# A Strassen second product in a pooled-attention and GELU-MLP kernel on one core

## The chip, the core and the metric

The kernel runs on one core of a Trainium2 chip. TensorE (PE) multiplies matrices and writes only to PSUM; VectorE (DVE), ScalarE (ACT) and GpSimd (POOL) do elementwise work, each from its own queue in program order; SyncE's queue (SP) issues nearly all DMAs, also in order. The metric is the device time of the core in microseconds, lower is better.

## The reference

For each of 8 batches with 8 heads, 576 queries of 64 elements attend to keys and values that are averaged over runs of 8 (72 pooled keys per head). The result, 4608 tokens of 512, goes through an MLP with 2048 hidden units and a tanh GELU.

```python
k_p = k.reshape(B, H, Sp, pool, D).mean(axis=3)
v_p = v.reshape(B, H, Sp, pool, D).mean(axis=3)
scores = scale * np.matmul(q, k_p.transpose(0, 1, 3, 2))
attn = softmax(scores)                       # over the 72 pooled keys
x = np.matmul(attn, v_p)                     # then (B*S, H*D)
h = x @ w_in                                 # 512 -> 2048
g = 0.5 * h * (1.0 + np.tanh(c * (h + 0.044715 * h * h * h)))
out = g @ w_out                              # 2048 -> 512
```

## The kernel before

**Tiling.** The tokens go in nine groups of 512. Groups 0 to 7 are the first 512 tokens of a batch each; the ninth, R, gathers the last 64 tokens of all eight batches. The order is `seq = [0, 1, ..., 6, R, 7]`; below, "group n" counts places in this order, 0 to 8. Weights stay in SBUF as bf16 (`w_in_b`, `w_out_b`), and so does the hidden activation of the current group, `gT` (128 partitions x 16 chunks x 512 tokens). Everything of the reference is computed with bf16 matmuls into float32 PSUM.

**A group's MLP**, `mlp` (line 368). First product: for each of 16 chunks `fo` of the hidden units, `hidden` (340) issues 4 matmuls of 512 columns into one PSUM bank, and ACT writes the GELU into `gT` (346). Second product: for each of 4 quarters of the tokens, 16 matmuls of 512 columns (`output`, 360) with `gT` as the stationary operand, then a VectorE copy out of PSUM (`finish`, 363) and a store. Group 0 has its own order (`mlp_first`), which works in token halves of 256 columns (`hidden_half`, 348) in its first product. The last group cuts its last quarter into column pieces (line 388).

**Work of the next group in between.** `mlp` calls `hook(s)` ahead of matmul number s of the group (its *slot*: 0 to 63 in the first product, 64 to 127 in the second), and what is registered there is emitted at this place in the program order of all engines. The schedule is written by hand (`manual_schedule`), so that a slot fixes the order in each engine's queue, and semaphores do the rest. The attention of group n+1 is registered in group n as follows:

- slot 12 (26 in group 1): `pool(b, 0, 5)`, three float32 additions on VectorE (132 to 134) of k and the first part of v over the 8 elements of a run, `dup_k`, and the transpose of the pooled keys by DMA from SP (184);
- slot 32: `pool(b, 5, 9)`, and at 33 `spread_v` on GpSimd (154), which lays the pooled v out block-diagonally in `vbd`;
- slot 56: `k_spread`, two VectorE copies into `kbd`; slot 57: the load of q for group n+2;
- slots 67, 69, 78, 82: four `scores` (214, 4 matmuls each) and `exps` on ACT (229); the PSUM tag `sc` has two tiles;
- slots 79, 82, 86, 90: four `norm` (sum 236, reciprocal 245, multiply 248; the second one's multiply on GpSimd), each followed by a DMA transpose of the result from SP (278);
- slot 91: `cast_q` of group n+2 on GpSimd, its DMA transpose (205), and `load_kv` of group n+2, the load of k and v (99, 94, 92); slot 92: a part of R's q (115);
- slot 121: `values` (298), 16 matmuls of 512 columns (310; for R 64 of 64 columns, 319), and two ACT copies into `xT`, the moving operand of the next group's first product.

Each pooling uses the kv tile that was loaded in the group before. Groups 1 to 5 load such a tile; group 7 needs no pooling, since the batch of the last group was pooled for R. The PSUM tag `mm` has four banks, which hidden chunks and output quarters take in turn.

**Staging.** `w_in` and `w_out` arrive as float32 in tiles of the tag `kv` (three buffers, shared with the k and v loads) and are cast to bf16 during group 0.

Of the kernel before, what the change touches and what calls it, by code (L numbers as in the profile page):

```python
# [19 lines left out]
def kernel(  # L20
# [36 lines left out]
    kvp = ctx.enter_context(tc.tile_pool(name="kvp", bufs=3))  # L57
# [168 lines left out]
    def exps(g, j):  # L226
        sc = st[g].pop(("sc", j))
        e = work.tile([128, H, Sp], F32, name="e", bufs=4)
        nc.scalar.activation(out=e.rearrange("p (x h) s -> p x (h s)", x=2), in_=sc[:, :, 0:4 * Sp],  # L229
                             func=ACT.Exp, scale=1.0 / 64.0)  # L230
# [49 lines left out]
    def xT_tile(g):  # L280
        st[g]["xT"] = work.tile([128, KO, MAIN], BF16, name="xT")
# [81 lines left out]
    def finish(g, r, o, eng):  # L363
        osb = work.tile([128, DM], F32, name="osb", bufs=4)
        copy(eng, osb, o)
        store(g, r, osb)

    def mlp(g, hooks, last):
# [5 lines left out]
        for r in range(4):  # L374
            if last and r == 3:
                break
            o = psum.tile([128, DM], F32, name="mm", tag="mm", bufs=4)
            for fo in range(FO):
                hook(64 + 16 * r + fo)
                output(g, r, fo, o)  # L380
            finish(g, r, o, nc.vector)
        if last:

            osb = work.tile([128, DM], F32, name="osb", bufs=4)
            for i, (c0, c1) in enumerate([(0, 256), (256, 384), (384, 512)]):
                o = psum.tile([128, DM], F32, name="mm", tag="mm", bufs=4)
                for fo in range(FO):
                    nc.tensor.matmul(out=o[:, 0:c1 - c0], lhsT=gT[:, fo, 384:512], rhs=w_out_b[:, fo, c0:c1],  # L388
                                     start=(fo == 0), stop=(fo == FO - 1))
                copy(nc.vector, osb[:, c0:c1], o[:, 0:c1 - c0])  # L390
                store(g, 3, osb, c0, c1, nc.scalar if i == 1 else nc.sync)
# [211 lines left out]
    for n_, g in enumerate(seq):  # L603
        if n_ == 0:
            continue
        hooks = {}
        if n_ + 1 < len(seq):
# [16 lines left out]
            for j in range(4):  # L624
                sj = ([67, 67, 80, 80] if n == R else [67, 69, 78, 82])[j]
                at(hooks, sj, scores, n, j)
                at(hooks, sj, exps, n, j)
# [4 lines left out]
            tail_of_attention(hooks, n, 121)
        if n_ + 2 < len(seq):
# [4 lines left out]
            at(hooks, 91, cast_q, n2, 0, 4, nc.gpsimd)  # L638
            at(hooks, 91, qT_tile, n2)
            at(hooks, 91, q_transpose_dma, n2)  # L640
            at(hooks, 91, load_kv, n2)
        if n_ == 1:
            at(hooks, 92, q_tile, R)
        if 1 <= n_ <= 4:
            at(hooks, 92, load_q, R, n_ - 1, n_, nc.sync)
        mlp(g, hooks, n_ + 1 == len(seq))
# [30 lines left out]
```

The softmax here doesn't subtract the row's maximum and nothing guards it: scores larger than these inputs give would overflow.

## Time and profile before

| | us |
|---|---|
| median of 3 runs | 294.53 (294.53 to 294.56) |
| span of the profiled execution | 292.6 |
| group 0's start to the first matmul of group 1 | 52.1 |
| first matmul of groups 2, 3, 4, 5, 6 | 82.14, 111.98, 141.83, 171.73, 201.57 |
| first matmul of groups 7 and 8 | 232.05, 261.89 |
| first 128-column piece of the last group to the last matmul's end | in 286.06 to 289.76 |
| granted TensorE clock | 1.000 |
| VectorE busy in group 3, first and second product | 7.13 of 13.82, 8.52 of 16.03 |
| GpSimd busy in group 3, first and second product | 2.51, 3.51 |

The span is the time from the first to the last instruction of one profiled execution; the runs' times include what lies around it. The lines of a timeline below give start, length, engine, kernel line, operation, output and inputs with shapes, and the count of instructions merged; in brackets stands how long the engine sat idle before it, and what ended that. `SPq` is the SP queue's issue of a DMA. `PEld` is a weight load.

### The profile page before, as it was taken

How to read it: one execution, taken by the hardware profiler on the slowest of the kernel's cores; microseconds unless marked ns; L12 is line 12 of the kernel's file. 1: busy time of each engine (PE TensorE's matmuls, PEld its weight loads, DVE VectorE, ACT ScalarE, POOL GpSimd, SP SyncE). 2: the span in 40 equal slices, each digit the busy share in tenths (PEclk: the TensorE clock that was granted, in tenths of full speed). 3: DMA queues.
4: the chain of work that ended last, by engine and by line, in shares of the span. 5: the costliest groups of instructions: out<-in, count | busy, mean ns of one | idle time of the engine just before them, and what ended most of it. 6: DMA issues, size and time to landing. Idle time of an engine off the chain costs nothing.

```text
span 292.6 us, 4562 instructions
## 1 busy us (share of the span) xinstructions
PE 284.2 (97%) x1712; PEld 142.8 (49%) x1739; DVE 141.8 (48%) x236; ACT 156.4 (53%) x233; POOL 64.7 (22%) x86
## 2 busy tenths in 40 slices
PE   8899999999999999999999999999999999999996
PEld 3678753445444544454445444544444544444444
DVE  5892778076517460757065806481639100920012
ACT  1586574777067706671567257724673377436500
POOL 4575443222303040114002400240024000100000
PEclk9999999999999999999999999999999999999999
DMA  7999999996699369945994599148944900451012
GB/s 234 354 386 347 380 381 201 340 257 168 149 298 278 102 134 288 251 142 133 268 283 150 126 250 299 15 113 243 293 146 103 183 23 2 85 112 38 0 72 72
DMA packets 73301, 56.32 MB, mean 192 GB/s; under 512 B 45888, under 2 KB 55488, under 8 KB 73280
## 3 DMA queue, kind: packets, MB, share of 16 engines
q1 hardware_dynamic: 73136, 55.98, 69.6%
q8 instruction: 13, 0.21, 0.3%
q10 hardware_dynamic: 144, 0.07, 0.1%
q14 instruction: 8, 0.07, 0.1%
HBM read 36.70 MB, written 9.44 MB: 158 GB/s over the span
## 4 chain that ended last, share of the span: by engine, by line
PE 81%; DMA 8%; DVE 4%; SPq 3%; ACT 1%; issue 1%; POOL 0%; ACTq 0%
PE mm L360 37%; PE mm L344 36%; DMA w_out_s<-in_moe_w_out_dram 5%; DMA w_in_s<-in_moe_w_in_dram 3%; PE xo L310 3%; PE sc L214 2%; SPq L437 2%; DVE eb L248 1%; ACT gT L346 1%; PE mm L388 1%; DVE den L236 1%; SPq L99 1%; PE xo L319 1%; DVE kv L132 0%; DVE kv L133 0%
## 5 line engine op out<-in xcount | busy, mean ns | idle before, releaser
L360 PE MATMUL mm<-w_out_b,gT 128*128 128x512 bf16 x543 | 125.9, 379 | 1.4 <-issue 0.8
L344 PE MATMUL mm<-xT,w_in_b 128*128 128x512 bf16 x502 | 111.4, 379 | 0.5
L346 ACT ACTIVATE gT<-mm 128x512 bf16<-128x512 f32 x128 | 76.4, 597 | 38.4 <-PE mm L344 38.4
L360 PEld LDWEIGHTS <-gT 128*128 128x128 bf16 x560 | 53.1, 98 | 60.3 <-issue 3.1
L344 PEld LDWEIGHTS <-w_in_b 128*128 128x128 bf16 x512 | 50.1, 98 | 60.5 <-issue 0.3
L81 DVE COPY osb<-mm 128x512 f32<-128x512 f32 (+2 forms) x37 | 24.2, 657 | 58.9 <-PE mm L360 52.8
L79 ACT CAST xT<-xo 128x1024 bf16<-128x1024 f32 (+1 forms) x18 | 16.6, 967 | 56.6 <-PE xo L310 48.2
L154 POOL TENSOR_TENSOR vbd<-kvb,vmask 128x256 bf16<-128x256 bf16 (+2 forms) x40 | 21.5, 561 | 105.1 <-DVE kvb L134 104.9
L236 DVE TENSOR_REDUCE den<-e 128x8 f32<-128x576 f32 x36 | 26.5, 736 | 36.8 <-ACT e L229 36.8
L132 DVE TENSOR_TENSOR kv<-kv 128x1024 f32<-128x1024 f32 (+3 forms) x19 | 21.8, 1149 | 38.4 <-DMA kv<-in_v_dram 32.3
L229 ACT ACTIVATE e<-sc 128x576 f32<-128x576 f32 x36 | 22.4, 650 | 9.6 <-ACT e L229 4.1
L248 DVE TENSOR_TENSOR eb<-e,r 128x576 bf16<-128x576 f32 x24 | 23.3, 972 | 0.8
L81 POOL CAST q_b<-q_sb 128x2048 bf16<-128x2048 f32 (+2 forms) x9 | 17.4, 1937 | 14.5 <-DMA q_sb<-in_q_dram 14.5
L248 POOL TENSOR_TENSOR eb<-e,r 128x576 bf16<-128x576 f32 x6 | 6.9, 1150 | 57.3 <-ACT e L229 30.4
L355 PE MATMUL mm<-xT,w_in_b 128*128 128x256 bf16 x128 | 15.5, 273 | 0.2 <-DVE xT L81 0.2
L214 PE MATMUL sc<-kbd,qT 128*128 128x144 bf16 x128 | 13.3, 226 | 0.4 <-ACT qT L79 0.2
L214 PEld LDWEIGHTS <-qT 128*128 128x128 bf16 x128 | 9.9, 98 | 7.3 <-issue 0.7
L355 PEld LDWEIGHTS <-w_in_b 128*128 128x128 bf16 x128 | 12.1, 98 | 1.8 <-issue 0.3
L133 DVE TENSOR_TENSOR kv<-kv 128x512 f32<-128x512 f32 (+3 forms) x19 | 12.4, 651 | 0.7
L357 ACT ACTIVATE gT<-mm 128x512 bf16<-128x512 f32 x16 | 9.5, 597 | 5.9 <-PE mm L355 5.8
L558 ACT ACT_TABLE_LOAD x8 | 10.3, 1283 | 0.1
L81 POOL CAST w_in_b<-w_in_s 128x512 bf16<-128x512 f32 (+1 forms) x10 | 8.6, 874 | 2.4 <-DMA w_in_s<-in_moe_w_in_dram 2.4
(62 smaller groups left out, 123.5 us busy)
## 6 DMA issues: line engine op xcount, KB each, us to landing
out_dram<-osb SPq DMA_DIRECT2D x31, 256.0 KB, 6.8
kv<-in_k_dram SPq DMA_DIRECT2D x7, 1024.0 KB, 7.6
q_sb<-in_q_dram SPq DMA_DIRECT2D x7, 1024.0 KB, 6.2
kv<-in_v_dram SPq DMA_DIRECT2D x6, 1024.0 KB, 9.2
w_in_s<-in_moe_w_in_dram SPq DMA_DIRECT2D x8, 512.0 KB, 9.8
w_out_s<-in_moe_w_out_dram SPq DMA_DIRECT2D x4, 1024.0 KB, 13.7
kv<-in_v_dram SPq DMA_DIRECT2D x4, 512.0 KB, 10.2
out_dram<-osb SPq DMA_DIRECT2D x9, 128.0 KB, 2.4
```

The costliest lines, as they stand in the source:

```text
L79: eng.copy(out=out, in_=in_)
L81: eng.tensor_copy(out=out, in_=in_)
L132: add(out=t[:, :, 0:4, :], in0=t[:, :, 0:4, :], in1=t[:, :, 4:8, :], op=ALU.add)
L154: eng.tensor_tensor(out=vbd[p0:128, b, n0:n1, :].rearrange("p (c r) (hh d) -> p c (r hh) d", c=max(m, 1), d=D), in0=kvb[p0:128, 4 + c0:4 + ...
L214: nc.tensor.matmul(out=o, lhsT=qT[:, j, pr, :], rhs=kbd[:, g, pr].rearrange("d hh s -> d (hh s)"), start=True, stop=True)
L229: nc.scalar.activation(out=e.rearrange("p (x h) s -> p x (h s)", x=2), in_=sc[:, :, 0:4 * Sp], func=ACT.Exp, scale=1.0 / 64.0)
L236: nc.vector.reduce_sum(out=den, in_=e, axis=AX.X)
L248: eng.tensor_tensor(out=o.rearrange("p (h s) -> p h s", s=Sp), in0=e, in1=r.unsqueeze(2).to_broadcast([128, H, Sp]), op=ALU.mult)
L344: nc.tensor.matmul(out=hp, lhsT=w_in_b[:, ko, fo * 128:(fo + 1) * 128], rhs=st[g]["xT"][:, ko, :], start=(i == 0), stop=(i == KO - 1))
L346: nc.scalar.activation(out=gT[:, fo, :], in_=hp, func=ACT.Gelu_apprx_tanh)
L355: nc.tensor.matmul(out=hp[:, f, :], lhsT=w_in_b[:, ko, (fo + f) * 128:(fo + f + 1) * 128], rhs=st[g]["xT"][:, ko, c0:c0 + 256], start=(ko ...
L360: nc.tensor.matmul(out=o, lhsT=gT[:, fo, r * 128:(r + 1) * 128], rhs=w_out_b[:, fo, :], start=(fo == 0), stop=(fo == FO - 1))
```

## The change

**The second product of groups 1 to 8** is computed by Strassen's scheme in Winograd's form. `gT` is seen as a 2 x 2 matrix of blocks: token halves (256 columns each) by even and odd chunks (a11, a12 for the first half, a21, a22 for the second). `w_out_b` likewise: even and odd chunks by left and right 256 output columns (b11 to b22). Instead of 64 matmuls of 512 columns there are seven products, in the order 1, 2, 6, 5, 7, 3, 4, of 2 x 8 matmuls of 256 columns each, so that the second product has 112 slots (64 to 175).

- `w_sums` builds four sums of w_out's blocks once (`tw`): two on GpSimd at slot 168 of group 0, two on VectorE at slots 2 and 6 of group 1.
- `g_sums` builds, for each group and each pair of chunk pairs, s3 = a11 - a21, s1 = a21 + a22 (in place, over a21), s2 = s1 - a11 and s4 = a12 - s2: four bf16 additions of 2 x 256 elements, at slots 18, 34, 50 (all on VectorE) and 65 (s3 on GpSimd).
- Three PSUM banks accumulate: x takes products 1, 6, 7, 4; y takes 2; z takes 5, 3. Between them VectorE and ACT copy intermediate sums into `keep` or add them into `osb`: x after 1 (VectorE) and after 6 (ACT), z after 5 (ACT). Output goes out in two stores per group, after products 3 and 4.

**The first product of groups 2 to 8** begins with its first four chunks by token halves (`hidden_half`, 32 matmuls of 256 columns), then goes on in 512. **The values** are cut into halves to match (`values_part`): the first half at slot 156 of the group before, the second at slot 4 of the group itself, and each is copied by ACT and VectorE, one half each.

**Slots and buffers.** The attention's slots in the second product are spread over the new count: scores at 68, 71, 92, 100; norms at 81, 97, 104, 114; cast of q, q's transpose and `load_kv` at 116. The tag `kv` has two buffers instead of three, and a constant tile `stage` takes the second half of each weight and later the sums s2 to s4 and `keep`. `kvb` and `xT` have one buffer instead of two, `e` three instead of four.

```diff
-    kvp = ctx.enter_context(tc.tile_pool(name="kvp", bufs=3))
+    kvp = ctx.enter_context(tc.tile_pool(name="kvp", bufs=2))
...
+    NP = FO // 2
+    HN = DM // 2
+    tw = consts.tile([128, 4, NP, HN], BF16, name="tw")
+    stage = consts.tile([128, 4096], F32, name="stage")
+    sums_ = stage[:, 0:3072].bitcast(BF16).rearrange("p (i m t) -> p i m t", i=3, m=NP)
+    keep = stage[:, 3072:4096].rearrange("p (i c) -> p i c", i=2)
+    wq = w_out_b.rearrange("p (m e) c -> p m e c", e=2)
+    gq = gT.rearrange("p (m e) t -> p m e t", e=2)
...
-            st[b]["kvb"] = work.tile([128, NB, 2, D], BF16, name="kvb")
+            st[b]["kvb"] = work.tile([128, NB, 2, D], BF16, name="kvb", bufs=1)
...
-        e = work.tile([128, H, Sp], F32, name="e", bufs=4)
+        e = work.tile([128, H, Sp], F32, name="e", bufs=3)
...
-        st[g]["xT"] = work.tile([128, KO, MAIN], BF16, name="xT")
+        st[g]["xT"] = work.tile([128, KO, MAIN], BF16, name="xT", bufs=1)
...
+    def values_part(g, half, engs):
+
+        xo = psum.tile([128, 2, 2, 256], F32, name="xo", tag="sc", bufs=2)
+        eT = st[g]["eT"]
+        for x in range(2):
+            if g < B:
+                for part, rows_ in ((SMALL, 32), (BIG, 64)):
+                    for pr in (x, x + 2):
+                        for hh in range(2):
+                            r0, c = part[2 * pr + hh]
+                            n = dict(PARTS[pr])[c]
+                            nc.tensor.matmul(out=xo[64 * hh:64 * hh + 64, pr // 2, x, :],
+                                             lhsT=vbd[r0:r0 + rows_, g, n, 64 * hh:64 * hh + 64],
+                                             rhs=eT[r0:r0 + rows_, 2 * half:2 * half + 2, c, :],
+                                             start=(part is SMALL), stop=(part is BIG))
+                continue
+            for pr in (x, x + 2):
+                for b in range(4 * half, 4 * half + 4):
+                    p0 = 64 * (b % 2)
+                    t0 = 64 * (b - 4 * half)
+                    for y, (c, n) in enumerate(PARTS[pr]):
+                        nc.tensor.matmul(out=xo[:, pr // 2, x, t0:t0 + 64], lhsT=vbd[:, b, n, :],
+                                         rhs=eT[:, b // 2, c, p0:p0 + 64], start=(y == 0), stop=(y == 1))
+        for k in range(2):
+            copy(engs[k], st[g]["xT"][:, 2 * k:2 * k + 2, 256 * half:256 * half + 256], xo[:, k])
...
+    def osb_tile():
+        return work.tile([128, 2, DM], F32, name="osb")
...
+    def w_sums(which, m0, m1, eng):
+
+        b11, b12, b21, b22 = [wq[:, m0:m1, i, HN * h:HN * h + HN] for i in range(2) for h in range(2)]
+        t = [tw[:, i, m0:m1] for i in range(4)]
+        in0, in1 = [(b12, b11), (b22, t[0]), (b22, b12), (b21, t[1])][which]
+        eng.tensor_tensor(out=t[which], in0=in0, in1=in1, op=ALU.subtract)
+
+    def g_sums(m0, eng3):
+
+        a11, a12, a21, a22 = [gq[:, m0:m0 + 2, i, 256 * h:256 * h + 256] for h in range(2) for i in range(2)]
+        s2, s3, s4 = [sums_[:, i, m0:m0 + 2] for i in range(3)]
+        eng3.tensor_tensor(out=s3, in0=a11, in1=a21, op=ALU.subtract)
+        nc.vector.tensor_tensor(out=a21, in0=a21, in1=a22, op=ALU.add)
+        nc.vector.tensor_tensor(out=s2, in0=a21, in1=a11, op=ALU.subtract)
+        nc.vector.tensor_tensor(out=s4, in0=a12, in1=s2, op=ALU.subtract)
...
+    def mlp(g, hooks, last, split):
         hook = runner(hooks)
-        for fo in range(FO):
+        if split:
+            for half in range(2):
+                for fo in (0, 2):
+                    hidden_half(g, fo, half, lambda s: hook(s // 2) if s % 2 == 0 else None, 16 * half + 4 * fo)
...
+        y, z = bank(), bank()
+        x = psum.tile([128, 2, MAIN], F32, name="x2", tag="sc", bufs=2)[:, :, 0:HN] if last else bank()
+        osb = [osb_tile(), osb_tile()]
+        add = nc.vector.tensor_tensor
+        lhs = {1: (gq, 0, 0), 2: (gq, 1, 0), 4: (gq, 1, 256), 5: (gq, 0, 256)}
+        for n, (prod, acc, fresh) in enumerate([(1, x, 1), (2, y, 1), (6, x, 0), (5, z, 1), (7, x, 0), (3, z, 0), (4, x, 0)]):
+            for p in range(2):
+                for m in range(NP):
+                    hook(64 + 16 * n + 8 * p + m)
+                    if prod in lhs:
+                        t, e, c = lhs[prod]
+                        lt = t[:, m, e, c + 128 * p:c + 128 * p + 128]
+                    else:
+                        lt = sums_[:, {6: 0, 7: 1, 3: 2}[prod], m, 128 * p:128 * p + 128]
+                    rt = {1: lambda: wq[:, m, 0, 0:HN], 2: lambda: wq[:, m, 1, 0:HN], 3: lambda: wq[:, m, 1, HN:DM],
+                          4: lambda: tw[:, 3, m], 5: lambda: tw[:, 0, m], 6: lambda: tw[:, 1, m], 7: lambda: tw[:, 2, m]}[prod]()
+                    nc.tensor.matmul(out=acc[:, p, :], lhsT=lt, rhs=rt, start=bool(fresh and m == 0 and (p == 0 or (last and acc is x))),
+                                     stop=(m == NP - 1), skip_group_check=True)
+                if last and prod == 4:
+                    copy(nc.vector, osb[1][:, p, 0:HN], x[:, p])
+                    nc.sync.dma_start(out=out[g * S:g * S + MAIN, :].rearrange("(t j) c -> t j c", j=4)[:, 2 + p, 0:HN],
+                                      in_=osb[1][:, p, 0:HN])
+            left, right = [slice(HN * i, HN * i + HN) for i in range(2)]
+            k0, k1 = [keep[:, i].rearrange("p (r c) -> p r c", r=2) for i in range(2)]
+            if prod == 1:
+                copy(nc.vector, k0, x)
+            elif prod == 2:
+                add(out=osb[0][:, :, left], in0=y, in1=k0, op=ALU.add)
+            elif prod == 6:
+                copy(nc.scalar, k0, x)
+            elif prod == 5:
+                copy(nc.scalar, k1, z)
+            elif prod == 7:
+                add(out=osb[1][:, :, right], in0=x, in1=k1, op=ALU.add)
+                if last:
+                    store_pair(g, 1, osb[1], HN, DM)
+            elif prod == 3:
+                add(out=osb[0][:, :, right], in0=z, in1=k0, op=ALU.add)
+                store_pair(g, 0, osb[0])
+            elif not last:
+                copy(nc.vector, osb[1][:, :, left], x)
+                store_pair(g, 1, osb[1])
...
+    for which in (0, 2):
+        at(hooks, 168, w_sums, which, 0, NP, nc.gpsimd)
...
+        for i in range(4):
+            at(hooks, [18, 34, 50, 65][i], g_sums, 2 * i, nc.gpsimd if i == 3 else nc.vector)
+        if n_ == 1:
+            at(hooks, 2, w_sums, 1, 0, NP, nc.vector)
+            at(hooks, 6, w_sums, 3, 0, NP, nc.vector)
...
-                sj = ([67, 67, 80, 80] if n == R else [67, 69, 78, 82])[j]
+                sj = 64 + ([4, 4, 30, 34] if n == R else [4, 7, 28, 36])[j]
                 at(hooks, sj, scores, n, j)
                 at(hooks, sj, exps, n, j)
                 if j == 0:
-                    at(hooks, 79, eT_tile, n)
-                at(hooks, [79, 82, 86, 90][j], norm, n, j, nc.gpsimd if j == 1 else nc.vector)
-                at(hooks, [79, 82, 86, 90][j], e_transpose_dma, n, j)
-            tail_of_attention(hooks, n, 121)
+                    at(hooks, 64 + 17, eT_tile, n)
+                nj = 64 + [17, 33, 40, 50][j]
+                at(hooks, nj, norm, n, j, nc.gpsimd if j == 1 else nc.vector)
+                at(hooks, nj, e_transpose_dma, n, j)
+            at(hooks, 64 + 66, nc.scalar.preload_act_table_set, GELU_SET)
+            at(hooks, 64 + 92, xT_tile, n)
+            at(hooks, 64 + 92, values_part, n, 0, [nc.scalar, nc.vector])
+        if n_ > 1:
+            at(hooks, 4, values_part, g, 1, [nc.scalar, nc.vector])
...
-            at(hooks, 91, cast_q, n2, 0, 4, nc.gpsimd)
-            at(hooks, 91, qT_tile, n2)
-            at(hooks, 91, q_transpose_dma, n2)
-            at(hooks, 91, load_kv, n2)
+            at(hooks, 64 + 52, cast_q, n2, 0, 4, nc.gpsimd)
+            at(hooks, 64 + 52, qT_tile, n2)
+            at(hooks, 64 + 52, q_transpose_dma, n2)
+            at(hooks, 64 + 52, load_kv, n2)
...
-        mlp(g, hooks, n_ + 1 == len(seq))
+            at(hooks, 64 + 53, load_q, R, n_ - 1, n_, nc.sync)
+        mlp(g, hooks, n_ + 1 == len(seq), n_ > 1)
```

More of the change, by code (lines that the diff above doesn't have):

```diff
@@ L363, in finish, with store_pair @@
     def finish(g, r, o, eng):
[L364 to L368, printed above, removed]
-        hook = runner(hooks)
-        for fo in range(FO):
+        osb = osb_tile()
+        copy(eng, osb[:, 0, :], o)
+        store(g, r, osb[:, 0, :])
+    def osb_tile():
+        return work.tile([128, 2, DM], F32, name="osb")
+    def store_pair(g, half, osb, c0=0, c1=DM, eng=nc.sync):
+        if g < B:
+            dst = out[g * S:g * S + MAIN, :].rearrange("(p j) c -> p j c", j=4)[:, 2 * half:2 * half + 2, c0:c1]
+            eng.dma_start(out=dst, in_=osb[:, :, c0:c1])
+        else:
+            for b in range(4):
+                r0 = (4 * half + b) * S + MAIN
+                p0 = 64 * (b % 2)
+                eng.dma_start(out=out[r0:r0 + 64, :], in_=osb[p0:p0 + 64, b // 2])
+    def w_sums(which, m0, m1, eng):
[11 more added lines that the diff above has]
+    def mlp(g, hooks, last, split):
+        hook = runner(hooks)
+        if split:
+            for half in range(2):
+                for fo in (0, 2):
+                    hidden_half(g, fo, half, lambda s: hook(s // 2) if s % 2 == 0 else None, 16 * half + 4 * fo)
+        for fo in range(4 if split else 0, FO):
             hidden(g, fo, hook, 4 * fo)
@@ L373, in mlp, with bank @@
             nc.scalar.preload_act_table_set(EXP_SET)
[L374 to L391, printed above, removed]
+        def bank():
+            return psum.tile([128, 2, HN], F32, name="mm", tag="mm", bufs=4)
@@ new lines, in mlp @@
+        y, z = bank(), bank()
[10 more added lines that the diff above has]
+                        lt = t[:, m, e, c + 128 * p:c + 128 * p + 128]
+                    else:
+                        lt = sums_[:, {6: 0, 7: 1, 3: 2}[prod], m, 128 * p:128 * p + 128]
[27 more added lines that the diff above has]
+                store_pair(g, 1, osb[1])
@@ L433 @@
         if c % 2 == 0:
-            w_in_s.append(kvp.tile([128, KO, 1024], F32, name="w_in_s", tag="kv"))
+            w_in_s.append(kvp.tile([128, KO, 1024], F32, name="w_in_s", tag="kv") if c == 0 else
+                      stage.rearrange("p (k f) -> p k f", k=KO))
         o = 512 * (c % 2)
@@ L448, in w_out_load @@
         if c % 2 == 0:
-            w_out_s[c // 2] = kvp.tile([128, 8, DM], F32, name="w_out_s", tag="kv")
+            w_out_s[c // 2] = (kvp.tile([128, 8, DM], F32, name="w_out_s", tag="kv") if c == 0 else
+                               stage.rearrange("p (f c) -> p f c", f=8))
         t = w_out_s[c // 2][:, 4 * (c % 2):4 * (c % 2) + 4, :]
@@ L637 @@
                 at(hooks, 57, load_q, n2, 0, 4, nc.sync)
[L638 to L641 removed]
+            at(hooks, 64 + 52, cast_q, n2, 0, 4, nc.gpsimd)
+            at(hooks, 64 + 52, qT_tile, n2)
+            at(hooks, 64 + 52, q_transpose_dma, n2)
+            at(hooks, 64 + 52, load_kv, n2)
         if n_ == 1:
[L643 removed]
+            at(hooks, 64 + 53, q_tile, R)
         if 1 <= n_ <= 4:
[L645 to L646 removed]
+            at(hooks, 64 + 53, load_q, R, n_ - 1, n_, nc.sync)
+        mlp(g, hooks, n_ + 1 == len(seq), n_ > 1)
 _INS = ['q', 'k', 'v', 'moe_w_in', 'moe_w_out']
```

## The prediction

> **What bounds the kernel now.** I read the page's busy shares first, then the timelines of the four engines and of the SP queue over one middle group. The page says:
>
> ```profile
> PE 284.2 (97%) x1712; PEld 142.8 (49%) x1739; DVE 141.8 (48%) x236; ACT 156.4 (53%) x233; POOL 64.7 (22%) x86
> ```
>
> PE is busy nearly all the time, VectorE (DVE) half. TensorE's timeline of group 3, and the one stretch where 256-column matmuls run alone (start, length, engine, line, count):
>
> ```profile
> 23.06 9.01 PE L355 MATMUL mm<-xT,w_in_b 128*128 128x256 bf16 x81
> ...
> 109.35 1.18 PE L310 MATMUL xo<-eT,vbd 32*64 32x512 bf16 x16
> 110.46 1.69 PE L360 MATMUL mm<-w_out_b,gT 128*128 128x512 bf16 x7
> 111.98 13.98 PE L344 MATMUL mm<-xT,w_in_b 128*128 128x512 bf16 x62
> 125.80 0.81 PE L360 MATMUL mm<-w_out_b,gT 128*128 128x512 bf16 x3
> 126.44 0.41 PE L214 MATMUL sc<-kbd,qT 128*128 128x144 bf16 x4
> ```
>
> The first product takes 125.80 - 111.98 = 13.82 us for 64 matmuls, 0.216 each. The group's period is 29.85 (111.98 to 141.83). A 256-column matmul costs (9.01 - 0.27, the last one's length) / 80 = 0.109, with a weight load for each: the load stays hidden. PE has no gap, so PE bounds this kernel. But VectorE and the SP queue run in a loop beside it, and the reader should see how little slack that loop has. First the SP queue (issues), then VectorE:
>
> ```profile
> 107.68 1.33 SPq L205 DMA_TRANSPOSE qT<-q_b  x1
> 109.06 1.30 SPq L99 DMA_DIRECT2D kv<-in_k_dram  x1
> ...
> 133.24 4.18 SPq L278 DMA_TRANSPOSE eT<-eb  x3
> 137.52 1.71 SPq L205 DMA_TRANSPOSE qT<-q_b  x1
> 139.28 1.20 SPq L99 DMA_DIRECT2D kv<-in_k_dram  x1
> ```
>
> ```profile
> 117.71 1.49 DVE L132 TENSOR_TENSOR kv<-kv 128x1280 f32<-128x1280 f32 x1 [4.83 <-DMA kv<-in_v_dram]
> ...
> 120.80 1.42 DVE L132 TENSOR_TENSOR kv<-kv 128x1024 f32<-128x1024 f32 x1
> 122.25 0.69 DVE L133 TENSOR_TENSOR kv<-kv 128x512 f32<-128x512 f32 x1
> ...
> 124.82 0.93 DVE L81 COPY kbd<-kTd 64x288 bf16<-64x288 bf16 x2 [1.42 <-DMA kTd<-kvb]
> 128.65 0.75 DVE L236 TENSOR_REDUCE den<-e 128x8 f32<-128x576 f32 x1 [2.90 <-ACT e L229]
> ...
> 134.83 1.36 DVE L248 TENSOR_TENSOR eb<-e,r 128x576 bf16<-128x576 f32 x1
> ```
>
> The loop: the kv load is issued at 109.06; VectorE waits 4.83 us for it and pools from 117.71; scores, exponentials and four norms follow, the last ending at 134.83 + 1.36 = 136.19; the SP queue, in order, issues the last transpose of e, then that of q (137.52), and only then the next kv load at 139.28. Load to load is 30.2 us, of which only 1.42 + 2.90 = 4.3 are waits that can close up. The bare loop is thus 25.9 us, against a PE period of 29.85.
>
> **What the Trainium skill says.** "VectorE: DVE Perf Modes", section on the perf-mode tier table: an all-bf16 tensor_tensor out of SBUF runs two elements a cycle, 1224 ns for 2048 elements against 2293 ns in float32. The trace has no all-bf16 tensor_tensor on VectorE; its float32 one of 512 elements (0.69 us) and of 1280 (1.49) fit the page's one-a-cycle rate with about 151 cycles fixed. "SBUF — State Buffer", section "Who interferes with whom": a VectorE instruction with two SBUF inputs and a GpSimd instruction that reads SBUF exclude each other. The trace agrees: the norm's multiply takes 0.76 alone and 1.36 beside GpSimd's 2.42 us cast of q. "TensorE: Matmul & The Clock Gate", section "Back-to-back issue gap": 262 cycles for 256 columns, the 0.109 above.
>
> **The change, part by part.**
>
> *TensorE.* 64 matmuls of 0.216 (13.82) become 112 of 0.109 (12.23): -1.59 a group, eight groups, -12.7. The first four chunks of the first product, in halves, are 32 x 0.109 instead of 16 x 0.216: +0.04, seven groups, +0.3. The values: 16 matmuls took 1.11 (109.35 to 110.46); now 32 of half the columns, between 0.56 and 1.11 per 16; I take 0.6, so +0.1 a group, +0.7. Unhindered, a middle group is 29.85 - 1.59 + 0.04 + 0.1 = 28.4 us.
>
> *ACT.* Two PSUM copies more, 0.60 each by the 512-element rows, and half of the xT copy goes to VectorE: it has 1 us or so to spare at each product. Nothing. *PSUM.* Bank x is read out after products 1 and 6 while products 2 and 5 (1.75 us each) run; enough for a 0.69 copy if the copying engine is free.
>
> *VectorE, the part that decides.* g_sums adds 15 additions of 512 bf16 elements (one more on GpSimd, about 1.0 from its 576-element row of 1.15, hidden unless VectorE is early). Bounds: 0.33 if the fixed part is 58 cycles (the same page's errata table), 0.69 if the float32 rate held. I take (256 + 151) / 0.96 = 0.42, and 0.45 start to start, since s1, s2 and s4 depend on each other: 1.8 for four, 1.35 for three. They stand in VectorE's program order behind the pooling from group 2 on: slot 12 pools, slots 18, 34 and 50 are sums, slot 65 the last sums. So they can't fill the wait for kv. They are queued behind it, and behind them stand k_spread, the copy of product 1, the norms, and through SP the next kv load. The kv load still stands behind the norms and q's transpose (slot 116 against 114). The new loop, in order:
> - kv issue to pooling 8.4 (117.71 - 109.06 = 8.65 here; five groups give 7.4 to 9.2)
> - pooling of five chunks 3.1 (117.71 to 120.80), sums 1.8, pooling of four 2.6
> - sums beside spread_v, which holds GpSimd 2.1 us: 1.8 + 0.3 (0 to 1.6); sums 1.8
> - k_spread 0.8; last three sums 1.35
> - copy of product 1: 0.65
> - norms with one PSUM eviction among them 7.5 (128.65 to 136.19)
> - last e transpose 1.3, q transpose 1.8 (136.19 to 139.28 = 3.1)
>
> Sum 33.2. The short way agrees: 25.9 + 6.75 + 0.65 = 33.3. This exceeds the 28.4 that PE needs, so the loop sets the pace. PE will be seen waiting in product 6, which needs s2 and the emptied bank x: they come about 4.5 us late. That wait could lower the granted clock afterwards (the page's clock-gate part names idle windows of some 3.4 us); PE then has slack, so it costs 0 to 1.7 us once, at the end of the loop; I take 0.
>
> *GpSimd and group 1.* w_sums puts two 2048-element additions on GpSimd, about 3.7 us each by the slope between its 256- and 576-element rows, from 49.9 to 57.3; VectorE's two w_sums need their results and end near 58.6, just as the kv data lands (58.58). Then: sums 1.8, pooling 3.1, sums 1.8, pooling 2.6, sums 2.1, k_spread 0.8, sums 1.35, copy 0.65, norms 7.5, SP 3.1: the kv load goes out at 83.4 (before: 79.78). If w_sums are free: 81.6.
>
> *Stores, tile counts.* Fewer, larger stores behind the loads as before; buffers cut from 3 to 2 or 2 to 1 are released a group earlier than needed (kv(n+2) overwrites a tile pooled in the preceding group). Nothing; if that cover were missing, a load would be later still.
>
> *Sum.* Loads go out in groups 1 to 5; the loop repeats four times: 83.4 + 4 x 33.2 = 216.2. The sixth group pools 7.7 later (no part of the remainder's q is loaded with it) and reaches the emptied bank after 3.1 + 1.8 + 2.6 + 2.1 + 1.8 + 0.8 + 1.35 + 0.65 = 14.2, at 238.1; five products of 1.75, scores and the remainder's 32 value matmuls (half of 2.03) are 10.1: 248.2, where before stood 232.05. The seventh (no pooling) runs at PE's pace, 28.9 with its own value matmuls: 277.1. The last is 13.85 + 0.6 + 12.23 = 26.7: 303.8. The tail, before 292.6 - 289.76 = 2.9: span 306.7. The median of the runs is 294.53 - 292.6 = 1.9 above the profiled span: **308.6 us**.
>
> **Rivals.**
> A, faster: the loop hides under PE. Then 294.5 - 12.7 + 0.3 + 0.7 = 282.8. It needs a loop below 28.4, 4.8 us less than my sum. For it: VectorE is only 48% busy, and with 15 x 0.45 more per group some 70%. Against: busy share counts for nothing in a chain that waits 8.4 us for its data. The kernel becomes faster than before where the loop is below about 30.6, since the end moves some 5.5 us per us of loop and mine lies 14.1 above the old time.
> B, the loop binds but barely: additions at 0.33 (-1.8), loads at 7.4 (-1.0), no GpSimd interference (-0.3): 30.1, giving about 291.5; with the middle of these, 31.5, about 299. For it: each end is within its bounds. Against: all at once.
> C, the additions run at the float32 rate, 0.69 + 0.04: +4.2 per loop, 37.4: 308.6 + 5.5 x 4.2 = 332. For it: the pattern is two runs of 256 with a gap, and one is in place. Against: both runs are contiguous 16-bit.
> D: PE's 256-column stream in the second product does not hide its weight loads (98 ns each): against it stands 0.109 over 81 matmuls with the same kind of loads.
>
> **How the numbers follow.** The forecast (loop 32 to 35, 302 to 318) has 0.62; A 0.10; B 0.14, of which 0.03 is faster, 0.02 the same and the rest slower; C 0.12; D 0.02. The range 297 to 325 takes in B's upper half and the interference bound of 1.6 (x 5.5 = 9), and leaves out A and most of C. Within 0.2% (0.6 us) is about what a measurement can't tell from no change. Faster 0.13, same 0.02, slower 0.85.
>
> **What would show it.** In the changed kernel's trace: 256-column matmuls at 0.109 in the second product; a PE gap of 3 to 5 us per group before product 6, released by VectorE; VectorE without idle time from pooling to the last norm; the kv load issued after the group's end instead of 2.9 us ahead of it, and 33 us from the one before; bf16 additions at 0.42. I am wrong if PE runs through (A), if additions are 0.69 (C), or if the kv load goes out before the norms.

## The result, and the profile after

The changed kernel takes 341.07 us (median of four runs, 339.48 to 341.83), the kernel before 294.53 on the same chip: 1.157 times as long, 95% interval 1.153 to 1.160. The forecast said slower, by 14; it is 46.5. The profiled execution spans 340.0 us against 292.6. The page of the changed kernel:

```profile
PE 294.6 (87%) x2289; PEld 200.4 (59%) x2299; DVE 215.6 (63%) x379; ACT 161.0 (47%) x249; POOL 86.0 (25%) x96
...
PE   8889994697999499948999699939998699999995
...
DVE  5875680597738784396739773888449954483532
...
PEclk9999998597999789996999799969999599999999
...
DVE 35%; PE 32%; DMA 20%; SPq 8%; issue 4%; POOL 1%; ACT 1%; DVEq 0%; POOLq 0%
```

The first line is busy time by engine, the next three are the span in 40 slices (tenths busy, and the granted TensorE clock), the last is the chain that ended last, by engine. TensorE (PE) held 81% of that chain before and holds 32% now; VectorE (DVE) and DMA hold 55%. In groups 1 to 6 PE falls to between 3 and 6 tenths, and the clock falls there or in the slice behind. The first such hole, in slices 7 and 8, is the widest.

The windows view, one line for group 1, one for group 2 and one for group 7 (stretch, its length, busy time of PE, PEld, DVE, ACT and GpSimd with counts, granted clock, DMA share, GB/s):

```profile
52.44:95.06 42.62, 32.14 (x209) 19.92 (x208) 26.73 (x43) 17.31 (x27) 15.34 (x11) 0.84 0.52 140
95.06:132.41 37.35, 32.06 (x241) 22.10 (x240) 24.96 (x42) 17.07 (x26) 7.91 (x8) 0.91 0.66 164
278.83:308.35 29.52, 29.16 (x258) 21.07 (x257) 16.89 (x33) 16.96 (x26) 2.30 (x2) 1.00 0.21 59
```

Groups 1 to 8 took 30.04, 29.84, 29.85, 29.90, 29.84, 30.48, 29.84 and 30.71 us before. After, they take 42.62, 37.35, 37.99, 35.07, 37.11, 36.25, 29.52 and 31.65. So group 1 gives +12.6, groups 2 to 6 give +33.9, groups 7 and 8 together +0.6, and the start +0.3: 47.4. Group 7, which pools nothing, is the only one that gained. The loss lies in two places, the loop of groups 2 to 6 and a separate delay in group 1.

**The loop.** SP's issues around the second product of group 2, then VectorE, then PE:

```profile
93.85 1.29 SPq L108 DMA_DIRECT2D kv<-in_k_dram  x1
...
122.10 7.56 SPq L287 DMA_TRANSPOSE eT<-eb  x4
129.77 1.81 SPq L214 DMA_TRANSPOSE qT<-q_b  x1
131.63 1.11 SPq L108 DMA_DIRECT2D kv<-in_k_dram  x1
```

```profile
102.77 1.49 DVE L141 TENSOR_TENSOR kv<-kv 128x1280 f32<-128x1280 f32 x1 [4.38 <-DMA kv<-in_v_dram]
...
106.50 0.42 DVE L429 TENSOR_TENSOR gT<-gT 128x512 bf16<-128x512 bf16 x1
...
113.40 1.19 DVE L429 TENSOR_TENSOR gT<-gT 128x512 bf16<-128x512 bf16 x1
...
115.42 0.46 DVE L90 COPY kbd<-kTd 64x288 bf16<-64x288 bf16 x2
...
119.66 0.69 DVE L90 COPY stage<-mm 128x512 f32<-128x512 f32 x1 [2.40 <-PE mm L463]
```

```profile
110.33 0.60 PE L463 MATMUL mm<-w_out_b,gT 128*128 128x256 bf16 x4
115.94 0.64 PE L223 MATMUL sc<-kbd,qT 128*128 128x144 bf16 x4 [5.01 <-DVE kbd L90]
...
117.49 4.38 PE L463 MATMUL mm<-w_out_b,gT 128*128 128x256 bf16 x21
...
129.28 1.00 PE L345 MATMUL xo<-eT,vbd 32*64 32x256 bf16 x16
130.22 0.61 PE L463 MATMUL mm<-w_out_b,stage 128*128 128x256 bf16 x4
```

The kv load goes out at 131.63, 0.8 us ahead of the group's end at 132.41 (2.9 ahead before), and 37.8 us after the one before it (30.2). VectorE waits for the load, pools, and works without a gap to 117.3. PE issues four matmuls of product 1 and then stops for 5.01 us, ahead of the scores and not ahead of product 6: the scores need `kbd`, and k_spread stands behind two rounds of sums in VectorE's order. Soon after the stop, 21 matmuls of 256 columns take from 117.49 to 121.70, 4.2 us, where 21 x 0.109 is 2.3. VectorE in turn stands idle for 2.40 us until PE has finished product 1. So each of the two waits for the other once per group.

**Group 1.** The waits view of the changed kernel (who waits for whom: us in all, times, the longest), summed over the whole span:

```profile
DVE xT L90 <- ACT xT L88: 25.4, 14, 2.1
...
PE sc L223 <- DVE kbd L90: 23.2, 5, 6.1
...
DVE stage L90 <- PE mm L463: 10.9, 5, 2.4
...
DVE osb L90 <- DMA out_dram<-osb: 11.3, 1, 11.3
...
PE mm L379 <- DVE osb L90: 7.9, 1, 7.9
```

The second and third lines are the loop's pair: five times in five groups. The last two occur once, at 50 to 62 us. Group 0's four output evictions went into four `osb` tiles before; now each takes one of two tiles of twice the size. The third waits 11.3 us for the store of the tile that it takes over, which stands in SP's queue behind the kv load, and PE waits 7.94 us for the PSUM bank that this eviction would empty.

### The profile page after: what moved, and what is told of

The parts are those of the page before. It is cut to its first block, busy times and chain, and to the rows that moved or that the text cites. A ratio compares the mean times of both kernels' runs of the same rounds, so it can differ in the third digit from the quotient of the medians.

```text
span 340.0 us, 5749 instructions
## 1 busy us (share of the span) xinstructions
PE 294.6 (87%) x2289; PEld 200.4 (59%) x2299; DVE 215.6 (63%) x379; ACT 161.0 (47%) x249; POOL 86.0 (25%) x96
## 4 chain that ended last, share of the span: by engine, by line
DVE 35%; PE 32%; DMA 20%; SPq 8%; issue 4%; POOL 1%; ACT 1%; DVEq 0%; POOLq 0%
PE mm L463 16%; DMA kv<-in_v_dram 10%; PE mm L379 7%; DVE kv L141 5%; DMA kv<-in_k_dram 4%; DVE gT L429 4%; DVE den L245 4%; DVE eb L257 3%; DMA out_dram<-osb 3%; DVE kv L142 3%; DVE stage L430 3%; SPq L214 3%; DMA q_sb<-in_q_dram 2%; SPq L108 2%; DVE stage L428 2%
## 5 line engine op out<-in xcount | busy, mean ns | idle before, releaser
L379 PE MATMUL mm<-xT,w_in_b 128*128 128x512 bf16 x392 | 89.5, 385 | 8.5 <-DVE osb L90 7.9
L379 PEld LDWEIGHTS <-w_in_b 128*128 128x128 bf16 x400 | 39.7, 99 | 55.6 <-issue 11.4
L390 PE MATMUL mm<-xT,w_in_b 128*128 128x256 bf16 x352 | 43.4, 273 | 1.8 <-DVE xT L90 1.8
L463 PEld LDWEIGHTS <-stage 128*128 128x128 bf16 x384 | 37.4, 100 | 9.6 <-issue 4.2
L392 ACT ACTIVATE gT<-mm 128x512 bf16<-128x512 f32 x44 | 26.2, 597 | 33.3 <-PE mm L390 33.3
L463 PE MATMUL mm<-w_out_b,gT 128*128 128x256 bf16 x240 | 38.9, 319 | 0.0
L390 PEld LDWEIGHTS <-w_in_b 128*128 128x128 bf16 x352 | 33.5, 98 | 7.5 <-issue 3.2
L463 PE MATMUL mm<-tw,stage 128*128 128x256 bf16 x224 | 29.6, 283 | 4.0 <-DVE stage L90 4.0
L463 PE MATMUL mm<-tw,gT 128*128 128x256 bf16 x240 | 29.3, 276 | 0.0
L245 DVE TENSOR_REDUCE den<-e 128x8 f32<-128x576 f32 x36 | 26.4, 734 | 2.3 <-ACT e L238 2.3
L90 DVE CAST xT<-xo 128x512 bf16<-128x512 f32 x16 | 11.1, 691 | 26.1 <-ACT xT L88 25.4
L223 PEld LDWEIGHTS <-qT 128*128 128x128 bf16 x128 | 11.3, 108 | 26.4 <-issue 24.1
L429 DVE TENSOR_TENSOR gT<-gT 128x512 bf16<-128x512 bf16 x32 | 18.7, 586 | 9.8 <-POOL stage L428 5.1
L88 ACT CAST xT<-xo 128x512 bf16<-128x512 f32 (+1 forms) x18 | 11.3, 634 | 22.3 <-PE xo L345 14.7
L428 POOL TENSOR_TENSOR stage<-gT 128x512 bf16<-128x512 bf16 x8 | 10.1, 1261 | 42.8 <-ACT gT L381 42.8
## 6 DMA issues: line engine op xcount, KB each, us to landing
kv<-in_v_dram SPq DMA_DIRECT2D x4, 512.0 KB, 10.2
```

What stands on the lines that cost most here:

```text
L223: nc.tensor.matmul(out=o, lhsT=qT[:, j, pr, :], rhs=kbd[:, g, pr].rearrange("d hh s -> d (hh s)"), start=True, stop=True)
L245: nc.vector.reduce_sum(out=den, in_=e, axis=AX.X)
L379: nc.tensor.matmul(out=hp, lhsT=w_in_b[:, ko, fo * 128:(fo + 1) * 128], rhs=st[g]["xT"][:, ko, :], start=(i == 0), stop=(i == KO - 1))
L390: nc.tensor.matmul(out=hp[:, f, :], lhsT=w_in_b[:, ko, (fo + f) * 128:(fo + f + 1) * 128], rhs=st[g]["xT"][:, ko, c0:c0 + 256], start=(ko ...
L392: nc.scalar.activation(out=gT[:, fo:fo + 2, c0:c0 + 256], in_=hp, func=ACT.Gelu_apprx_tanh)
L429: nc.vector.tensor_tensor(out=a21, in0=a21, in1=a22, op=ALU.add)
```

## The experiments

All ratios are to the kernel before, on the same chip. Unless said otherwise a kernel is the changed one with the edit shown.

**1. Four output tiles for group 0.** Its evictions go into the halves of two tiles, so that none waits for a store.

```diff
+    first_osb = {}
+
     def finish(g, r, o, eng):
-        osb = osb_tile()
-        copy(eng, osb[:, 0, :], o)
-        store(g, r, osb[:, 0, :])
+        if r % 2 == 0:
+            first_osb[r // 2] = osb_tile()
+        osb = first_osb[r // 2][:, r % 2, :]
+        copy(eng, osb, o)
+        store(g, r, osb)
```

> The changed kernel with group 0's four output evictions placed in the two halves of two osb tiles (four places, same memory) instead of one half of each of two tiles. Theory: the third and fourth eviction no longer wait 11 us for a store that stands behind the kv load, so group 1's matmuls run through: the 7.9 us PE gap at 54 to 62 us and the slow clock after it go, about 10 us, 341 to 331; the five groups from 2 on keep their 35 to 38 us. Rival (group 1 is late because GpSimd's two weight sums hold up VectorE): 341 stays within 2 us, and the gap only moves to the first sums.

Measured: 337.51 us, ratio 1.144 (1.140 to 1.149). Only 3.6 us of the 10 that were expected came back. The 7.94 us wait is gone. Now VectorE shows this:

```profile
54.24 7.89 DVE L426 TENSOR_TENSOR tw<-w_out_b,tw 128x2048 bf16<-128x2048 bf16 x2 [1.78 <-POOL tw L426]
```

PE:

```profile
75.49 0.64 PE L223 MATMUL sc<-kbd,qT 128*128 128x144 bf16 x4 [8.50 <-DVE kbd L90]
```

GpSimd:

```profile
50.15 8.08 POOL L426 TENSOR_TENSOR tw<-w_out_b 128x2048 bf16<-128x2048 bf16 x2
58.17 2.88 POOL L90 CAST q_b<-q_sb 128x2048 bf16<-128x2048 f32 x1
```

PE's wait at the scores grew from 2.33 to 8.50 us: in sum it waits 8.50 instead of 7.94 + 2.33 = 10.27. VectorE's two weight sums took 2.47 us in the changed kernel, where they ran after all of this GpSimd work, and take 7.89 here: the first ends at 59.3, after GpSimd's second sum, and the second at 62.1, after GpSimd's cast of q. Two delays lay one over the other, so that taking away one showed the other.

**2. The kv load at slot 2**, ahead of the norms in SP's order, instead of slot 116.

```diff
-            at(hooks, 64 + 52, load_kv, n2)
+            at(hooks, 2, load_kv, n2)
```

> The changed kernel with the kv load of group n+2 moved from slot 116 to slot 2 of the same group (its buffer is free by then), so that it no longer stands behind the norms and transposes. Theory (a loop from kv load over pooling, sums, k_spread, scores, product 1 and norms back to the kv load sets the pace of groups 2 to 6): the loop is cut, PE's waits at the scores go, and these groups fall from 35 to 38 us to about 29.5, the length of group 7; in all about 35 us less, 305 to 308. Rival A (VectorE simply has too much work in a group): periods stay above 33 us, in all above 325. Rival B (the load's own transfer is the bound): no change in the periods, or the transposes now wait for the load and eat half of the gain.

Measured: 314.68 us, ratio 1.065 (1.062 to 1.069): 26.4 less. The place of the load in the queue is most of the loop's cost, but some waiting is left. The waits view of this kernel:

```profile
PE sc L223 <- DVE kbd L90: 8.7, 5, 2.5
...
DVE kbd L90 <- DMA kTd<-kvb: 7.6, 5, 2.6
```

k_spread now waits for the transpose of the pooled keys, which it did not do in the changed kernel: the load was put ahead of that small transfer, which now takes 9.4 us from issue to landing (median of six) instead of 3.8.

**3. Both edits, 1 and 2.**

> Both edits, osb places and the early kv load. Theory: the two losses are independent, so the gains add: 341 - 10 - 35 = 296, within 2 us of the kernel before, since a group that waits for nothing takes 29.5 us against 29.84. Rival: with group 1 no longer late the gains overlap, and less than 40 us are recovered.

Measured: 311.97 us, ratio 1.054 (1.048 to 1.060), 16 above the expectation and about 3 below experiment 2. Group 1 still waits 8.51 us at its scores, as in experiment 1. The transpose of the keys for group 2 lands 10.2 us after its issue at 98.51, and k_spread waits 2.64 us for it. In the changed kernel, issued at 105.96, it landed after 3.7 us and was not waited for. (The trace is of the longest of the four runs, 315.15 us.)

**4. k_spread ahead of the middle sums**, slot 33 instead of 56, in groups 2 and on; the load stays late.

```diff
-                at(hooks, 56, k_spread, b, [nc.vector, nc.vector])
+                at(hooks, 33 if n_ > 1 else 56, k_spread, b, [nc.vector, nc.vector])
```

> The changed kernel with k_spread moved ahead of the second and third sums of a group (slot 33, right behind the pooling) in groups 2 to 6; nothing else. Theory (the period is 37 and not the forecast 33 because the scores at slot 68 wait for k_spread, which stands behind the sums, and then the copy of product 1 waits for PE): PE no longer stops at the scores but ahead of product 6, the 2.4 us idle of VectorE before the copy of product 1 goes, and each of the groups 2 to 5 loses 2.5 to 3 us: 341 to about 329. Rival (only VectorE's own work sets the period): no change, 341, or more by VectorE's wait for the transposed keys.

Measured: 331.16 us, ratio 1.124 (1.117 to 1.131), 9.9 less. PE, same group:

```profile
111.62 0.41 PE L223 MATMUL sc<-kbd,qT 128*128 128x144 bf16 x4 [0.18 <-DVE kbd L90]
...
118.61 1.01 PE L463 MATMUL mm<-tw,stage 128*128 128x256 bf16 x4 [3.01 <-DVE stage L90]
```

The wait at the scores is gone but for 0.6 us at most in groups 2 to 5, and PE stops 3.01 us ahead of product 6 instead. This is the picture that the prediction had drawn for the change itself, and groups 2 to 5 take 34.57, 34.13, 34.20 and 33.43 us, near its 33.2. So the link that it left out is k_spread to scores.

**5. All four weight sums on VectorE**, at slots 2 to 5 of group 1, with edit 1.

```diff
-    for which in (0, 2):
-        at(hooks, 168, w_sums, which, 0, NP, nc.gpsimd)
...
-            at(hooks, 2, w_sums, 1, 0, NP, nc.vector)
-            at(hooks, 6, w_sums, 3, 0, NP, nc.vector)
+            for which in range(4):
+                at(hooks, 2 + which, w_sums, which, 0, NP, nc.vector)
```

> The changed kernel with group 0's four osb places and with all four weight sums on VectorE, at slots 2 to 5 of group 1, instead of two on GpSimd in group 0. Theory: with the osb wait gone, VectorE's two weight sums took 7.9 us beside GpSimd's (8.1 us for two), and that kept group 1 late; four on VectorE alone take 4 x 1.22 = 4.9 us and end before the kv data lands near 58.6, so PE's first wait at the scores in group 1 falls from 8.5 to about 4 us and the whole run by 4 to 5 us against 337.5: about 333. Rival (VectorE's chain behind the landing of kv is what counts): within 1.5 us of 337.5.

Measured: 333.64 us, ratio 1.132 (1.130 to 1.134), 3.9 below experiment 1. Four sums on VectorE alone are done at 58.7, although one of them takes 2.79 us beside GpSimd's cast of q and the others 1.21 or 1.22; two on each engine were done at 62.1. Group 1's wait at the scores falls from 8.50 to 5.13.

**6. The kv load right behind the pooling**, so that the keys' transpose keeps its place ahead of it.

```diff
-            at(hooks, 64 + 52, load_kv, n2)
+            at(hooks, 27 if n_ == 1 else 13, load_kv, n2)
```

> The changed kernel with the kv load of group n+2 at slot 13 (27 in group 1), right behind the transpose of the pooled keys, and nothing else. Theory: with the load at slot 2 (314.7) the transposed keys came 10 us after their issue, behind the load, and k_spread waited 2.6 us for them; here they come in about 4 us as before, and PE's waits of 1 to 2.5 us at the scores shrink by some 1.5 us in five groups: about 307. Rival (the waits that were left come from the sums ahead of k_spread): 313 to 316. Rival (a transfer in flight delays the transposes of e that come later): above 316.

Measured: 309.80 us, ratio 1.050 (1.048 to 1.052): 31.3 less by one line, 4.9 more than by slot 2. SP and PE:

```profile
101.00 1.24 SPq L193 DMA_TRANSPOSE kTd<-kvb  x1
102.30 0.56 SPq L108 DMA_DIRECT2D kv<-in_k_dram  x1
```

```profile
111.15 0.41 PE L223 MATMUL sc<-kbd,qT 128*128 128x144 bf16 x4 [0.71 <-DVE kbd L90]
```

Of the loop 0.71 us a group is left, and groups 2 to 5 take 30.4 us. VectorE goes from the copy of `xT` straight to the pooling, and the keys' transpose lands 2.6 us after its issue. VectorE still does all its additions, so it was not their amount that made a turn of the loop so long.

**7. All of it**: edits 1, 5 and 6, and k_spread at slot 36 (48 in group 1).

> The changed kernel with four edits: four osb places in group 0, weight sums on VectorE in group 1, kv load at slot 13 (27 in group 1), k_spread at slot 36 (48 in group 1), ahead of the third sums. Theory: no PE wait over 0.5 us is left in any group, so every group from 1 on takes the 29.5 us of group 7 and the last one its 31.6: 52.4 + 28.2 + 6 x 29.5 + 31.6 = 289 span, 291 to 293 measured, 0.5 to 1.3% below the kernel before. Rival (VectorE's work, some 25 us a group, can't be packed without holding PE up): 296 to 303.

Measured: 294.96 us against 294.91, ratio 1.000 (0.999 to 1.001), 2 to 4 above the expectation. The waits of groups 2 to 6 are gone but for 0.2 to 0.3 us for `xT`, and the clock is 1.00, and still the kernel only draws level: a middle group takes 29.5 us, 0.3 less than before the change, where Strassen's product alone should give 1.59. Group 1 takes 31.9 us where 28.2 had been expected: it keeps a wait of 1.93 us at its scores and one of 1.14 ahead of product 6.

**8. The values in another order**, on top of 7: for each half all 32-row matmuls first and then all 64-row ones, into four PSUM banks instead of two, with each engine copying a tile of its own.

```diff
-        xo = psum.tile([128, 2, 2, 256], F32, name="xo", tag="sc", bufs=2)
+        xo = [psum.tile([128, 2, MAIN], F32, name="xo", tag="sc", bufs=2) for _ in range(2)]
...
-        for x in range(2):
-            if g < B:
-                for part, rows_ in ((SMALL, 32), (BIG, 64)):
-                    for pr in (x, x + 2):
+        if g < B:
+            for part, rows_ in ((SMALL, 32), (BIG, 64)):
+                for i in range(2):
+                    for pr in (i, i + 2):
...
-        for k in range(2):
-            copy(engs[k], st[g]["xT"][:, 2 * k:2 * k + 2, 256 * half:256 * half + 256], xo[:, k])
+        for i in range(2):
+            copy(engs[i], st[g]["xT"].rearrange("p (y i) t -> p i y t", i=2)[:, i, :, 256 * half:256 * half + 256],
+                 xo[i][:, :, 0:256])
```

> The kernel with the four edits, and the values' halves written as the kernel before wrote the whole: first all 32-row matmuls, then all 64-row ones, into four PSUM banks instead of two, each copied out by its own engine. Theory: 16 such matmuls took 0.94 us per half in the changed kernel against 1.11 for 16 of twice the columns before, because the order with only four matmuls between two into one bank leaves the row tiles less to overlap; in the old order a half takes about 0.6, so 0.7 us less in each of six groups, and the 0.22 us wait for xT goes too: 4 to 5 us below the kernel with four edits, about 287. Rival (each such matmul is bound by its own weight load, 16 x 0.058): 0.9 us per half stays, and only the xT wait goes, 1 to 1.5 us.

Measured: 289.50 us, ratio 0.982 (0.980 to 0.983): 1.8% faster than the kernel before, the best version of this study. PE, then the window of a middle group:

```profile
109.91 0.75 PE L345 MATMUL xo<-eT,vbd 32*64 32x256 bf16 x16
110.60 0.61 PE L469 MATMUL mm<-w_out_b,stage 128*128 128x256 bf16 x4
```

```profile
112.79:141.45 28.66, 28.61 (x241) 20.18 (x240) 24.03 (x42) 16.94 (x26) 7.83 (x8) 1.00 0.80 213
```

A half of the values takes 110.60 - 109.91 = 0.69 us (130.22 - 129.28 = 0.94 in the changed kernel). With two halves that is 0.5 a group, and the 0.22 us that PE waited for `xT` is gone too: together 0.72 of the 0.87 between 29.53 and 28.66. Order, banks and copies were changed together; which of them does it stays open. The last line shows a bound by PE again: 28.61 of 28.66 busy, with VectorE at 24.0.

**9. The clock.** Twenty matmuls of zeros ahead of the first scores of groups 2 to 5 fill PE's stop in the changed kernel.

```diff
+                if j == 0 and 2 <= n_ <= 5:
+                    at(hooks, sj, warm_up, 20, "sc")
                 at(hooks, sj, scores, n, j)
```

> The changed kernel with 20 matmuls of zeros (512 columns, 0.216 us each, 4.3 us, into a PSUM tile that nobody reads) put ahead of the first scores in groups 2 to 5, where PE otherwise idles 4 to 6 us. Theory: the idle time lowers the granted clock, product 1 then runs at half speed for some 3.5 us, and VectorE's copy of product 1, a link of the loop, waits 2.4 us for it; with PE kept busy that part runs at full clock, the copy comes 1 to 1.5 us sooner, and the run is 4 to 6 us shorter: 335 to 337. Rival (the slow clock lies in PE's slack, as forecast): 341 as before, or more where 4.3 us exceed the wait.

Measured: 334.38 us, ratio 1.134 (1.130 to 1.139), 6.7 less for added work. In the traces groups 2 to 5 together take 141.4 us instead of 147.5, 1.5 a group on average; a single group gains up to 2.3 or loses 0.4. PE, then VectorE:

```profile
109.44 4.48 PE L571 MATMUL warm<-zeros 128*128 128x512 bf16 x20
115.30 0.41 PE L223 MATMUL sc<-kbd,qT 128*128 128x144 bf16 x4 [1.38 <-DVE kbd L90]
...
116.13 2.46 PE L463 MATMUL mm<-w_out_b,gT 128*128 128x256 bf16 x21
```

```profile
117.31 0.69 DVE L90 COPY stage<-mm 128x512 f32<-128x512 f32 x1 [0.69 <-PE mm L463]
```

The 21 matmuls take 2.46 us instead of 4.38, and VectorE's wait falls from 2.40 to 0.69. The slow clock after the stop was inside the loop.

**10. The first sums of group 1 later**, slot 30 instead of 18, on top of 8.

> The kernel with the four edits and the reordered values, with the first sums of group 1 moved from slot 18 to slot 30, behind the pooling instead of ahead of it. Theory: group 1 is the one group where PE still waits (1.94 us at the scores, 1.14 ahead of product 6), because its kv data lands only 6 us into the group; pooling 1.8 us sooner takes most of the wait at the scores, not the one ahead of product 6: 1.5 to 2 us less, about 288. Rival (the wait just moves from the scores to product 6): 289.5 within 0.5 us.

Measured: 289.79 us, ratio 0.983 (0.982 to 0.984), no gain over experiment 8. Group 1's wait at its scores is 2.31 us (1.94 there), that ahead of product 6 still 1.14. What else holds group 1 was not followed further.

## Why the prediction was right in its direction and wrong in its size

Predicted span 306.7, measured 340.0. By the prediction's own milestones the 33.3 us between them are: the kv load of group 1 at 93.85 instead of 83.4, +10.5; four turns of the loop in 242.75 - 93.85 = 148.9 instead of 132.8, +16.1; the sixth group from its kv load to product 6 in 266.38 - 242.75 = 23.6 instead of 21.9, +1.7; from there to the seventh in 12.45 instead of 10.1, +2.4; the seventh group +0.6; the last with its tail +2.1 (these last two were not followed further).

**Right.** The change makes the kernel slower; the loop through VectorE and SP sets the pace of groups 2 to 6, and PE waits. An addition of 512 bf16 elements takes 0.42 us where GpSimd is quiet, so rival C (0.69) is out as a cause, though its 332 comes nearer by chance. The 256-column matmuls of the second product run at 0.109 (16 in 1.75), so rival D is out. Rivals A and B are out: no group from 2 to 6 ran at PE's pace. Experiments 2 and 6 confirm the mechanism, since moving the issue of the kv load alone gives back 26 and 31 us.

**The loop's list lacked a link.** The working ran "k_spread 0.8; last three sums 1.35", then "copy of product 1: 0.65", as if VectorE alone stood there. But scores come at slot 68, four matmuls into product 1, in PE's program order, and they need k_spread. So the copy comes after k_spread, scores and the rest of product 1: VectorE waits 2.40 us, the largest term of the 37.8 - 33.2 = 4.6 in the turn shown. These 2.40 are the link and the slow clock (below) together: in experiment 9, with the link in place and the clock full, 0.69 is left. For the same reason the stop was forecast ahead of product 6, and stands ahead of the scores. Group 6, whose first scores (those of R, at 258.38) run ahead of k_spread at 263.89, does show the forecast stop, 4.03 us ahead of product 6. Experiment 4 takes the link out and gets the forecast's picture and nearly its period.

**"I take 0" for the clock.** The Trainium skill, "TensorE: Matmul & The Clock Gate", Part 1, says that the array falls to half rate after an idle window of about 3.4 us. The trace agrees for the stop of 5.01 us, since the matmuls behind it run at about half rate. But it shows the same after a shorter stop, in group 1:

```profile
79.57 0.41 PE L223 MATMUL sc<-kbd,qT 128*128 128x144 bf16 x4 [2.33 <-DVE kbd L90]
...
80.39 4.12 PE L463 MATMUL mm<-w_out_b,gT 128*128 128x256 bf16 x21
```

So a stop below the page's 3.4 us was not safe here. The prediction knew of the slow clock, and argued that PE then has slack. It has none, because product 1 is in the loop. Experiment 9 puts the size at some 1.5 us a group, four times, against "0 to 1.7 us once". At the end of the loop, the one place that the prediction had in mind, it costs more than that too: behind the stop of group 6, products 6 and 5 with the scores between them take from 266.38 to 272.66, 6.3 us, where 32 x 0.109 and 0.3 for the scores make 3.8. That is the +2.4 above.

**Interference with GpSimd was mis-sized.** For the sums beside spread_v and the next ones the sum had 2.1 + 1.8; they took 112.68 - 110.09 = 2.59 and 115.42 - 112.68 = 2.74, together 1.4 more. The first addition of each of these rounds, then GpSimd in that stretch:

```profile
110.09 0.42 DVE L428 TENSOR_TENSOR stage<-gT 128x512 bf16<-128x512 bf16 x1
112.68 0.61 DVE L428 TENSOR_TENSOR stage<-gT 128x512 bf16<-128x512 bf16 x1
```

```profile
110.31 2.71 POOL L163 TENSOR_TENSOR vbd<-kvb,vmask 128x256 bf16<-128x256 bf16 x4 [4.13 <-DVE kvb L143]
112.98 1.33 POOL L428 TENSOR_TENSOR stage<-gT 128x512 bf16<-128x512 bf16 x1
```

The fourth addition of GpSimd's own, s3, had been counted as hidden; VectorE's 1.19 at 113.40 stands beside it. Against 1.8 for each round the excess is 1.7, just outside the bound of 1.6; the value taken was 0.3. This is read from the traces; no run took spread_v away. The other terms of that turn: the norms with their eviction 8.2 instead of 7.5 (0.55 of it a wait for PE), the load 8.9 instead of 8.4.

**Group 1: "Stores, tile counts ... Nothing" was wrong.** The prediction named kv, where the buffers cut were enough, and did not follow `osb` from four tiles to two of twice the size, of which group 0 uses half. "VectorE's two w_sums need their results and end near 58.6" was wrong as well: 62.1 in experiment 1, since each of VectorE's sums ended only after the GpSimd instruction beside it. Either delay covers much of the other; that is why experiment 1 gave 3.6 and not 10, and experiments 1 and 5 together 7.4. The start of group 1's pooling shows it: by the prediction's sum 58.6 + 1.8 = 60.4, in the changed kernel 67.91, in experiment 1 63.84, and in experiment 5, without both delays, 60.47. So 7.5 of the +10.5 are these two. The rest lies in the steps behind, where VectorE waits 1.70 us for product 1, the missing link again.

**The values: 0.6 for a half was 0.94**, inside the bounds (0.56 to 1.11). Two halves a group make that +0.77 instead of +0.1 against the old 1.11, and PE's wait for `xT` another 0.22. The cost of "half of the xT copy goes to VectorE ... Nothing" is that wait: VectorE's copy starts only when ACT's has ended. With that a group at PE's pace is 29.5 and not 28.4, and of the 1.59 that Strassen saves about 0.3 is left. Experiment 8, at 28.66, shows that 28.4 was nearly within reach.

**What could have been read beforehand.** That the scores need k_spread and stand inside product 1, and that group 0 has two output tiles instead of four, both stand in the diff and in the slots. The range, up to 325, took its width from the prices of the steps listed; a step that was not listed widened nothing.

## What to carry to other kernels

When a loop of waits is summed up, list what each step waits for on every engine's queue, also where the bounding engine is thought to have slack: here PE's own in-order queue closed the loop through k_spread, and a stop there was paid again in clock. When tiles are merged, count them anew for every user of the tag, also for the one that fills only half of each. Look at the place of an issue in a shared queue before the arithmetic: here one line returned 31 of the 46 us where it stayed behind the small transfer that others waited for, and 26 where it went ahead of it.

## What the runs showed of the hardware

- Two bf16 additions of 2048 elements on VectorE took 2.47 us with GpSimd idle, and 7.89 beside GpSimd (experiment 1): the first took 5.07 and ended 1.1 us after GpSimd's second addition, the other 2.79 and ended 1.1 us after GpSimd's cast of q. GpSimd's own two additions took 8.08 us there and 8.07 in the changed kernel, where VectorE stood idle beside them; its cast took 2.88 instead of 1.89. Splitting such work over both engines was slower than VectorE alone (four sums done at 62.1 against 58.7). The Trainium skill, "SBUF — State Buffer", section "Who interferes with whom", says that two such instructions exclude each other, and the trace agrees; the sizes are this case's.
- The DMA transpose of the pooled keys took 9.4 us from issue to landing (median of six) where it stood behind the kv load in SP's queue (experiment 2), 3.8 in the changed kernel, and 2.6 right ahead of the load (experiment 6).
- Sixteen matmuls of 256 columns on a part of the array took 0.94 or 0.69 us with the same operands and the same count, by the order of their row groups and the PSUM banks written, which were changed together.
- Where ACT and VectorE each copied one bank of one PSUM tile, VectorE began only when ACT had ended (ACT's copy of 0.59 us at 130.34, VectorE's at 130.95). With a tile for each they ran together (110.61 and 110.72 in experiment 8). No run tells whether the chip or the program's own semaphores kept them apart.
- Half rate of TensorE followed stops of 2.33 us (changed kernel, clock 0.57 from 80.39 to 84.35) and of 2.42 us (experiment 4, clock 0.50 from 187 to 190), but not one of 2.72 us in experiment 4 (clock 1.00 from 221.6 to 225). Twenty useless matmuls in the stops of groups 2 to 5 made the kernel 6.7 us faster.
